# Scheduler's timeline model switched off, and the turned tiles' fp16 halves moved from the transposed-tile pool to the untransposed one

## The chip, the cores and the metric

One core of one Trainium2 chip runs the whole program. The metric is the device time in microseconds. The time of before is the median of three runs; one further execution was profiled, and all rows below are of that one.

## The reference

The inputs are fp32 `q`, `k`, `v` of 2 batches x 8 heads x 768 positions x 64, a projection 64 x 6, and two pairs of feed-forward weights 512 x 2048 and 2048 x 512 in double precision.

```python
q_bits = (np.einsum('bhsd,dk->bhsk', q, proj) > 0)
q_bucket = np.sum(q_bits * powers, axis=-1)          # k likewise
mask = q_bucket[:, :, :, None] == k_bucket[:, :, None, :]
scores = np.where(mask, scale * np.matmul(q, k.T), -1e9)
attn = softmax(scores); x = (attn @ v), heads side by side: (1536, 512)
h = x @ w_in;  g = h * sigmoid(h);  x = g @ w_out     # first feed-forward
h = x @ w_in2; g = h - tanh(h);     out = g @ w_out2  # second feed-forward
```

Attention goes only between positions whose six hash bits agree; its result goes through two feed-forward layers.

## The kernel before

**Attention.** There are 16 heads, 8 of each batch, and each head has 6 score tiles of 128 query rows by 768 keys, so 96 tiles in all; they are counted here from 0, tile i being row block i % 6 of head i // 6. For one tile these steps follow each other:

- `scores` (line 243): four matmuls of 384 columns into two PSUM banks. Half of them need the head's hash rows, which `hash_mm` (line 172, PE), an eviction on DVE (line 185) and two small DMAs issued from ACT's queue (lines 187 and 188) have put into the operands beforehand.
- `soft_max` (line 256, DVE) reads the scores, takes the row maximum and writes the fp32 tile `p`; `soft_exp` (lines 264 and 265, ACT) makes the bias and the exponential in place.
- Then `p` is split into an fp16 high part and an fp16 rest, and both are transposed, in one of two ways. The 24 odd tiles of the first batch are turned on PE (`turn_p`, line 278): six transposes into PSUM, high part by ACT (line 280), rest by DVE (line 281). The 72 other tiles go by `soft_hi` (line 290, ACT), `soft_lo` (line 297, POOL) and a transposing DMA issued from SP's queue (line 299).
- `pv` (lines 311 to 313): 18 fp16 matmuls of 65 columns from the transposed tile `pt`, written in the source six tiles behind `scores`.

The loop over `s` issues these steps of several tiles staggered. Where a batch ends, 13 steps run without new scores.

**Pools.** `pt_p` has four buffers of 128 x 12 x 128 fp16; before, both ways put their transposed tile there. `wk` has four buffers for `p` and four for the fp16 pair `hl`. For the first 22 odd tiles (`EXTRA = 44`) `soft_max` takes a double-width fp32 tile from a pool that the feed-forward uses later (four buffers over two tags), with `p` in its first half and room for an fp16 pair in its second:

```python
big = extra.tile([128, 2 * S], F32, tag=("gh", "gl")[i // 2 % 2], name="p")
p = big[:, 0:S]
hlx[i] = big[:, S:2 * S].bitcast(F16).rearrange("p (a s) -> p a s", a=2)
```

Before, that second half stays unused.

**Feed-forward.** Weights of 512 x 512 pieces come in as pairs of 32-bit words, are turned to fp32 by ACT and four DVE steps (lines 506 to 510 and 497), split in two fp32r parts (lines 498 and 499), and those of the first layer are stored to DRAM as fp32 (line 501) for a second pass. A group is 12 matmuls of 384 columns into one bank (`h_group` line 530, `o_group` line 554) and an eviction by ACT and DVE (lines 536 to 542, 566). There are 256 groups. The first 64 belong to batch 0's tokens and are issued one per step beside the attention of batch 1; the other 192 follow it. While the two overlap, the scores have one buffer of two banks (`ps_s`), since the second was given to the feed-forward.

**Order.** The program is traced in the source's order, and the framework's scheduler then sets each engine's queue: it walks the program with a model of time and gives every engine the ready instruction of highest priority, the source's place being the priority (`@early` raises it for a few). Each engine, and SP's queue of DMAs, then executes its queue strictly in that order, held up by semaphores.

Of the kernel before, what the change touches and what calls it, by code (L numbers as in the profile page):

```python
# [9 lines left out]
F16 = mybir.dt.float16  # L10
# [39 lines left out]
def lsh_attention_moe_kernel(  # L50
# [12 lines left out]
    nc = tc.nc  # L63
    B, H, _, _, S = qkT.shape
# [4 lines left out]
    NQ = S // 128  # L69
# [34 lines left out]
    def bank():  # L104
        turn[0] += 1
        pool = ps_more[0] if ps_more and turn[0] % ps_turn[1] < ps_turn[0] else ps_m
        return pool.tile([128, 512], F32, tag="m", name="psm")


    def attention(pools, vraw, extra, xw):  # L110
# [9 lines left out]
        hlx, vmxs = {}, {}  # L120
# [148 lines left out]

        def turn_p(i):  # L270
            p, _ = pexp.pop(i)
            pt = pt_p.tile([128, 2 * NQ, 128], F16, tag="pt", name="pt")
            w = NQ // 2
            for u in range(2):
                ps = bank()
                for x in range(w):
                    kt = u * w + x
                    nc.tensor.transpose(ps[:, x * 128:(x + 1) * 128], p[:, kt * 128:(kt + 1) * 128], ident)
                hi, lo = (pt[:, x + u * w:x + (u + 1) * w, :].rearrange("p a q -> p (a q)") for x in (0, NQ))
                nc.scalar.copy(hi, ps[:, 0:HS])  # L280
                nc.vector.tensor_tensor(lo, ps[:, 0:HS], hi, op=ALU.subtract)
            ptile[i] = pt
# [88 lines left out]
        def at(s):  # L371
            b, r = divmod(s, per + gap)
            return b * per + r if s >= 0 and b < B and r < per else None

        for s in range(B * (per + gap)):
            evs, late = late, []
            i, i1, i2, j, j1, j3 = (at(s - x) for x in (0, 1, 2, LAG, LAG + 1, LAG + 2))
# [4 lines left out]
            if i2 is not None and direct(i2):  # L382
                turn_p(i2)
# [349 lines left out]
```

## Time and profile before

| | us |
|---|---|
| median of three runs | 794.8 |
| lowest and highest of them | 789.62, 795.64 |
| the profiled execution's own time | 791.22 |
| its span, first to last instruction | 789.4 |

Durations and gaps below are within the span of the profiled execution; 1.8 us of its time lie around the span. The trace divides into the attention of batch 0 alone (to about 154 us), batch 1's attention with the first 64 feed-forward groups (to about 390 us) and the other groups.

### The profile page before, as it was taken

Reading aid. Unit: us, or ns where it says so; the run is one execution under the profiler, and the core shown is the slowest. Engines: PE = TensorE matmul, PEld = TensorE weight load, DVE = VectorE, ACT = ScalarE, POOL = GpSimd, SP = SyncE. Lnnn points to the kernel's source line nnn. Section 1 sums busy time; section 2 is a strip of 40 time slices with the busy share of each in tenths; the row PEclk is TensorE's granted clock in tenths of the full one; section 3 lists DMA queues with packets and bytes.
Section 4 is the critical chain, followed back from the end, with each engine's and each line's share of the span. In section 5 each row is a group of like instructions: output and inputs, shape, how many; then the busy total and the mean of one; then the engine's idle time right before and its main releaser. Section 6 shows DMA issues by size and latency. Waiting matters only on the chain.

```text
span 789.4 us, 14334 instructions
## 1 busy us (share of the span) xinstructions
PE 733.6 (93%) x5492; PEld 700.0 (89%) x5492; DVE 544.4 (69%) x1029; ACT 433.1 (55%) x821; POOL 309.5 (39%) x214
## 2 busy tenths in 40 slices
PE   4778798789989899999999999999999999999998
PEld 3667677679978798899999999999999999999998
DVE  6968688798878778778542443998768576584342
ACT  4849788797788678667443441553524334242130
POOL 4536537466777667566455420222111110110000
PEclk8899899899999999999999999999999999999999
DMA  7695776969999899994333320323112121210102
GB/s 255 190 148 106 126 154 167 212 155 197 263 245 211 214 180 240 215 218 136 97 104 107 95 81 1 101 90 130 53 56 78 57 81 33 75 54 0 52 29 81
DMA packets 138879, 100.39 MB, mean 127 GB/s; under 512 B 115870, under 2 KB 118174, under 8 KB 138810
## 3 DMA queue, kind: packets, MB, share of 16 engines
q1 hardware_dynamic: 137712, 97.54, 50.6%
q10 hardware_dynamic: 1098, 1.94, 1.0%
q8 instruction: 43, 0.70, 0.3%
q14 instruction: 26, 0.21, 0.1%
HBM read 57.95 MB, written 11.53 MB: 88 GB/s over the span
## 4 chain that ended last, share of the span: by engine, by line
PE 55%; DMA 2%; ACT 1%; DVE 0%; issue 0%; POOL 0%; ACTq 0%; DVEq 0%
PE psm L554 28%; PE psm L530 26%; DMA pt<-hl 1%; DMA w<-wi 1%; PE ps L243 0%; ACT xh L577 0%; ACT p L265 0%; POOL hl L297 0%; PE pso L311 0%; POOL wl L485 0%; ACT wh L484 0%; ACT th L536 0%; PE pso L312 0%; PE pso L313 0%; ACT hl L290 0%
## 5 line engine op out<-in xcount | busy, mean ns | idle before, releaser
L499 POOL TENSOR_TENSOR wl<-wa,wh 128x512 fp32r<-128x512 f32 x64 | 83.8, 1309 | 244.3 <-ACT wh L498 244.3
L530 PE MATMUL psm<-xh,wh 128*128 128x384 f32 x512 | 173.2, 339 | 1.6 <-ACT wh L484 1.6
L554 PE MATMUL psm<-gh,wh 128*128 128x384 f32 x512 | 173.0, 338 | 0.6 <-ACT x L346 0.4
L554 PE MATMUL psm<-gl,wh 128*128 128x384 f32 x512 | 171.5, 335 | 0.0
L530 PE MATMUL psm<-xl,wh 128*128 128x384 f32 x512 | 171.4, 335 | 0.0
L530 PE MATMUL psm<-xh,wl 128*128 128x384 f32 x512 | 170.0, 335 | 0.0
L554 PE MATMUL psm<-gh,wl 128*128 128x384 f32 x512 | 169.4, 335 | 0.0
L297 POOL TENSOR_TENSOR hl<-p,hl 128x768 f16<-128x768 f32 x72 | 120.4, 1674 | 88.0 <-ACT hl L290 82.5
L256 DVE TENSOR_SCALAR_CACHE_REDUCE p<-ps 128x768 f32<-128x768 f32 x96 | 90.8, 952 | 29.7 <-PE ps L243 20.0
L530 PEld LDWEIGHTS psm<-xh,wh 128*128 128x128 f32 x512 | 96.5, 188 | 2.1 <-ACT wh L484 1.9
L243 PE MATMUL ps<-k,q 128*128 128x384 f32 x336 | 82.9, 372 | 15.9 <-DVE p L256 9.0
L554 PEld LDWEIGHTS psm<-gh,wh 128*128 128x128 f32 x512 | 96.3, 188 | 1.5 <-ACT x L346 0.6
L554 PEld LDWEIGHTS psm<-gl,wh 128*128 128x128 f32 x512 | 96.4, 188 | 0.0
L530 PEld LDWEIGHTS psm<-xl,wh 128*128 128x128 f32 x512 | 96.4, 188 | 0.0
L566 DVE TENSOR_TENSOR acc<-acc,psm 128x384 f32<-128x384 f32 x96 | 52.1, 551 | 63.5 <-PE psm L554 63.1
L530 PEld LDWEIGHTS psm<-xh,wl 128*128 128x128 f32 x512 | 95.9, 188 | 0.0
L554 PEld LDWEIGHTS psm<-gh,wl 128*128 128x128 f32 x512 | 95.8, 188 | 0.0
L542 DVE TENSOR_TENSOR gl<-psm,gh 128x384 fp32r<-128x384 f32 x128 | 70.6, 554 | 31.9 <-ACT gh L541 31.7
L265 ACT ACTIVATE p<-p,bi 128x768 f32<-128x768 f32 x96 | 89.0, 939 | 2.9
L541 ACT CAST gh<-psm 128x384 fp32r<-128x384 f32 x128 | 61.4, 480 | 50.5 <-DVE psm L540 35.1
L311 PE MATMUL pso<-v,pt 128*128 128x65 f16 x576 | 70.9, 200 | 15.4 <-DMA pt<-hl 15.3
L311 PEld LDWEIGHTS <-pt 128*128 128x128 f16 x576 | 55.3, 101 | 27.2 <-DMA pt<-hl 17.4
(90 smaller groups left out, 1267.2 us busy)
## 6 DMA issues: line engine op xcount, KB each, us to landing
w<-in_w_in_dram SPq DMA_DIRECT2D x32, 512.0 KB
w<-in_w_out_dram SPq DMA_DIRECT2D x32, 512.0 KB
r<-in_qkT_dram SPq DMA_DIRECT2D x15, 768.0 KB
wi<-wa SPq DMA_DIRECT2D x16, 256.0 KB
wo<-wa SPq DMA_DIRECT2D x16, 256.0 KB
w<-wi SPq DMA_DIRECT2D x16, 256.0 KB
w<-wo SPq DMA_DIRECT2D x16, 256.0 KB
vr<-in_v_dram SPq DMA_DIRECT2D x6, 512.0 KB
```

What stands on the lines that cost most here:

```text
L243: nc.tensor.matmul(out=ps[:, u, 0:HS], lhsT=a[:, t * 128:(t + 1) * 128], rhs=c[:, u * HS:(u + 1) * HS], start=(j == 0), stop=(j == 1))
L256: nc.vector.tensor_scalar(p.rearrange("p (c s) -> p c s", c=2), pss.pop(i)[:, :, 0:HS], FLOOR, None, op0=ALU.max, op1=ALU.max, accum_out=m)
L265: nc.scalar.activation(out=p, in_=p, func=ACTF.Exp, scale=0.125, bias=bi)
L297: nc.gpsimd.tensor_tensor(hl[:, 1, :], p, hl[:, 0, :], op=ALU.subtract)
L311: nc.tensor.matmul(out=o, lhsT=pt[:, kt, :], rhs=v16[:, kt, h, :], start=(kt == 0), stop=False)
L499: nc.gpsimd.tensor_tensor(ll, s, hh.bitcast(F32), op=ALU.subtract)
L530: nc.tensor.matmul(out=ps, lhsT=a[:, k, fs], rhs=b_[blk][:, k, :], start=(k == 0 and j == 0), stop=(k == KD - 1 and j == 2))
L541: nc.scalar.copy(gh[:, f, :], ps)
L542: nc.vector.tensor_tensor(gl[:, f, :], ps, gh[:, f, :].bitcast(F32), op=ALU.subtract)
L554: nc.tensor.matmul(out=ps, lhsT=a[:, f, ds], rhs=b_[:, f, :], start=(f == 0 and j == 0), stop=(f == F - 1 and j == 2))
L566: nc.vector.tensor_tensor(ac, ac, ps, op=ALU.add)
```

## The change

Two edits. The scheduler's model of time is switched from the timeline simulation to the simpler default, which changes the order on every queue. And `turn_p` no longer takes its fp16 tile from `pt_p`: it takes the unused second half of the odd tile's own buffer, or a `wk` buffer `hl` for the two odd tiles after `EXTRA`. From line 273 on, line numbers of the changed kernel are one higher.

```diff
         def turn_p(i):
             p, _ = pexp.pop(i)
-            pt = pt_p.tile([128, 2 * NQ, 128], F16, tag="pt", name="pt")
+            pt = hlx.pop(i) if i in hlx else wk.tile([128, 2, S], F16, tag="hl", name="hl")
+            pt = pt.rearrange("p a s -> p (a s)").rearrange("p (a q) -> p a q", q=128)
             w = NQ // 2
...
-    with _tile.TileContext(nc, schedule_with_timeline_sim=True) as tc:
+    with _tile.TileContext(nc, schedule_with_timeline_sim=False) as tc:
         lsh_attention_moe_kernel(tc, *args)
```

Neither setting gives the literal order of the source: of instructions that stand next to each other on a queue, 167 pairs on PE, 273 on DVE and 222 on ACT stood against the order in which the source issues them, and 92, 235 and 184 do now. The matmuls, evictions and DMAs themselves are the same in number and shape. In PE's queue of tiles 12 to 47 a `pv` stands on average 6.9 score tiles behind the newest scores (8.6 before), and in that of tiles 54 to 89 it stands 5.8 behind (3.9 before).

SP's queue, at the end of batch 0's attention, before: the transposing DMA of tile 38, two stores of converted weights (`wi32`) with the loads behind them, and the transposing DMAs of tiles 40 and 42.

```order
L299 DMA_TRANSPOSE pt_1898<-hl_1825 128x12x128
L501 DMA wi32_75<-wa_1563 128x512
L466 DMA w_1635<-in_w_in1_dram 128x1024
L501 DMA wi32_75<-wa_1586 128x512
L466 DMA w_1725<-in_w_in1_dram 128x1024
L299 DMA_TRANSPOSE pt_1979<-hl_1908 128x12x128
L299 DMA_TRANSPOSE pt_2076<-hl_1999 128x12x128
L134 DMA r_2568<-in_qkT_dram 128x1536
```

And the same place now, from the second store on; its transposing DMAs are those of tiles 38, 40 and 42.

```order
L502 DMA wi32_75<-wa_1570 128x512
L467 DMA w_1708<-in_w_in1_dram 128x1024
L300 DMA_TRANSPOSE pt_1879<-hl_1807 128x12x128
L502 DMA wi32_75<-wa_1641 128x512
L467 DMA w_1770<-in_w_out1_dram 128x1024
L300 DMA_TRANSPOSE pt_1959<-hl_1889 128x12x128
L502 DMA wi32_75<-wa_1714 128x512
L467 DMA w_1850<-in_w_out1_dram 128x1024
L300 DMA_TRANSPOSE pt_2055<-hl_1979 128x12x128
```

Four stores stand ahead of tile 42's transpose instead of two, and they alternate with the transposes.

ACT's queue in the middle of batch 0's attention, before: the two DMAs that carry head 5's hash rows (`h0_129`, `l0_130` from `hb`; the scores of tile 30 are the first that need them) stand behind the exponential of tile 25, `p_1200`.

```order
L264 ACTIVATE bi_1266<-mx_1232 128x1
L265 ACTIVATE p_1200<-p_1200,bi_1221 128x768
L280 CAST pt_1015<-psm_1016 128x384
L290 CAST hl_1185<-p_1144 128x768
L187 DMA h0_129<-hb_992 18x768
L280 CAST pt_1015<-psm_1022 128x384
L188 DMA l0_130<-hb_992 18x768
L280 CAST pt_1097<-psm_1098 128x384
```

Now the same two DMAs stand behind the exponential of tile 21, `p_1018`.

```order
L264 ACTIVATE bi_1120<-mx_1100 128x1
L281 CAST p_920<-psm_1006 128x384
L265 ACTIVATE p_1018<-p_1018,bi_1039 128x768
L281 CAST p_920<-psm_1012 128x384
L187 DMA h0_129<-hb_983 18x768
L188 DMA l0_130<-hb_983 18x768
L265 ACTIVATE p_1053<-p_1053,bi_1077 128x768
L281 CAST p_1018<-psm_1087 128x384
```

They moved four tiles forward against the exponentials; the high part of a turned tile (line 280, now 281) is written into the tile `p` itself.

DVE's queue beside the feed-forward, before: from the row maximum of tile 66 to that of tile 68 (`psm` and `gl` are a group's eviction, `cv` a weight conversion, `hb` a hash eviction).

```order
L256 TENSOR_SCALAR p_3406,mx_3407<-ps_3395 128x768
L537 SCALAR_TENSOR_TENSOR psm_3370<-th_3455,psm_3370 128x384
L542 TENSOR_TENSOR gl_3309<-psm_3312,gh_3308 128x384
L537 SCALAR_TENSOR_TENSOR psm_3442<-th_3530,psm_3442 128x384
L256 TENSOR_SCALAR p_3477,mx_3478<-ps_3467 128x768
L185 TENSOR_SCALAR hb_3577<-psm_3578,cst_sb_69 82x384
L507 TENSOR_SCALAR cv_3394<-cv_3394 128x512
L542 TENSOR_TENSOR gl_3309<-psm_3370,gh_3308 128x384
L542 TENSOR_TENSOR gl_3309<-psm_3442,gh_3308 128x384
L256 TENSOR_SCALAR p_3552,mx_3553<-ps_3542 128x768
```

Now the same stretch, tiles 66 to 68:

```order
L256 TENSOR_SCALAR p_3384,mx_3385<-ps_3373 128x768
L538 SCALAR_TENSOR_TENSOR psm_3348<-th_3433,psm_3348 128x384
L508 TENSOR_SCALAR cv_3372<-cv_3372 128x512
L256 TENSOR_SCALAR p_3455,mx_3456<-ps_3445 128x768
L509 TENSOR_SCALAR cv_3372<-cv_3372 128x512
L543 TENSOR_TENSOR gl_3287<-psm_3348,gh_3286 128x384
L511 SCALAR_TENSOR_TENSOR cv_3372<-w_3095,cv_3372 128x512
L538 SCALAR_TENSOR_TENSOR psm_3420<-th_3508,psm_3420 128x384
L498 SCALAR_TENSOR_TENSOR wa_3371<-w_3095,cv_3372 128x512
L256 TENSOR_SCALAR p_3530,mx_3531<-ps_3520 128x768
```

A whole weight conversion and a group's eviction now stand between the row maxima of tiles 67 and 68.

## Rows read from the trace of the kernel before

**Rows 1.** Page, part 1: busy time, share of the span and instructions

```profile
PE 733.6 (93%) x5492; PEld 700.0 (89%) x5492; DVE 544.4 (69%) x1029; ACT 433.1 (55%) x821; POOL 309.5 (39%) x214
```

**Rows 2.** Windows: stretch, its length, busy time per engine, granted clock, DMA share, GB/s

```profile
58.00:154.00 96.00, 79.26 (x948) 68.75 (x947) 75.20 (x159) 78.26 (x153) 53.86 (x32) 0.91 0.72 154
154.00:208.00 54.00, 49.38 (x420) 45.69 (x417) 49.37 (x94) 44.83 (x79) 36.64 (x24) 0.97 0.83 190
208.00:350.00 142.00, 133.89 (x1240) 122.63 (x1238) 111.67 (x219) 106.19 (x188) 92.29 (x60) 0.99 1.03 219
...
390.00:786.00 396.00, 395.84 (x2284) 395.52 (x2282) 237.46 (x426) 146.08 (x293) 77.94 (x60) 1.00 0.21 68
```

**Rows 3.** Lines 265 and 256, three stretches: count, duration, first and last start

```profile
L265 ACT ACTIVATE p<-p,bi x36: 919/936/970, 58.0 to 142.9; 128x768 f32<-128x768 f32 x36
...
L265 ACT ACTIVATE p<-p,bi x13: 930/939/966, 154.1 to 204.7; 128x768 f32<-128x768 f32 x13
...
L256 DVE TENSOR_SCALAR_CACHE_REDUCE p<-ps x35: 944/958/959, 208.1 to 350.0; 128x768 f32<-128x768 f32 x35
```

**Rows 4.** Chain that ended last: start, us, what

```profile
322.84 5.53 DMA pt<-hl
...
336.64 0.05 PE pso L311
...
337.19 0.25 PE psm L554
...
346.17 0.71 PE ps L243 x4
...
403.12 16.64 PE psm L554 x96
```

**Rows 5.** Waits, 58 to 154 us, PE and SP: total, times, longest

```profile
PE pso L311 <- DMA pt<-hl: 4.9, 2, 3.9
PE ps L243 <- DMA l<-hb: 3.5, 1, 3.5
PE ps L243 <- DMA k<-hb: 2.1, 3, 0.8
...
SPq L299 <- PE pso L313: 33.6, 11, 6.6
```

**Rows 6.** Timeline of SP's queue, 126 to 140 us

```profile
129.75 1.46 SPq L299 DMA_TRANSPOSE pt<-hl  x1
...
135.34 6.16 SPq L299 DMA_TRANSPOSE pt<-hl  x2
```

**Rows 7.** Timeline of ACT, 38 to 60 us

```profile
48.78 0.48 ACT L280 CAST pt<-psm 128x384 f16<-128x384 f32 x1 [4.25 <-PE psm L278]
```

**Rows 8.** Waits, 208 to 386 us, PE and SP

```profile
PE pso L311 <- DMA pt<-hl: 6.9, 6, 2.7
PE psm L530 <- ACT wh L484: 1.6, 1, 1.6
...
SPq L501 <- DVE wa L497: 22.2, 12, 4.4
```

**Rows 9.** Groups by form, 208 to 350 us, DVE: busy, mean ns, idle before

```profile
L256 DVE TENSOR_SCALAR_CACHE_REDUCE p<-ps 128x768 f32<-128x768 f32 x34 | 32.5, 954 | 14.5 <-PE ps L243 11.2 <-POOL wl L499 1.7 <-PE pso L313 1.4
...
L507 DVE TENSOR_SCALAR cv<-cv 128x512 f32<-128x512 f32 x18 | 12.5, 696 | 6.7 <-ACT cv L506 6.7
...
L537 DVE SCALAR_TENSOR_TENSOR psm<-th,psm 128x384 f32<-128x384 f32 x16 | 8.8, 554 | 0.1
L542 DVE TENSOR_TENSOR gl<-psm,gh 128x384 fp32r<-128x384 f32 x16 | 8.7, 548 | 0.9 <-ACT gh L541 0.9
```

**Rows 10.** Groups by form, 58 to 154 us, POOL and ACT

```profile
L297 POOL TENSOR_TENSOR hl<-p,hl 128x768 f16<-128x768 f32 x18 | 30.3, 1683 | 34.5 <-ACT hl L290 30.6 <-DMA k<-hb 3.9
...
L290 ACT CAST hl<-p 128x768 f16<-128x768 f32 x18 | 15.0, 835 | 1.0 <-DMA q<-hb 1.0
...
L163 POOL TENSOR_TENSOR k<-r,k 128x768 fp32r<-128x768 f32 x4 | 7.4, 1842 | 0.2
```

## The prediction

> **What bounds the kernel now.** I read the page's busy line first, then a table of stretches, then in each stretch the waits, and last the chain. PE is 93% busy [rows 1], but its share hides three regimes. Up to 154 us batch 0's attention runs alone: between 58 and 154 us no engine is full: PE shows 79.3 of 96 us, in matmuls that overlap, ACT 78.3 and DVE 75.2 [rows 2]. Between 208 and 350 us the attention of batch 1 shares PE with feed-forward groups; PE is busy 133.9 of 142 us. From 390 us on PE has 395.8 of 396 us, and the chain is nothing but groups of 12 matmuls, 16.64 us for 96 of them [rows 4], so 0.173 us for one of 384 columns. What stands there is work; no order of it can be cheaper. A gain has to come before 390 us, where an in-order queue waits for another.
>
> The marks in time are the exponentials and row maxima [rows 3]: the 13th exponential (tile 12) starts at 58.0 us, the 49th (tile 48, batch 1's first) at 154.1, the row maximum of tile 61 at 208.1 and of tile 95 at 350.0. I go from mark to mark.
>
> **Up to tile 12 (58.0 us): -3 us.** Two stops show what goes wrong here; the larger is ACT's 4.25 us before it copies a turned tile at 48.78, waiting for PE [rows 7], which itself stood in front of a `pv` whose transpose came late. The second edit leaves `pt_p` to the 72 tiles that go by DMA, and in SP's new queue the third transposing DMA no longer stands behind a load of q and k, so this stop should go: -4.25. Against it the new order puts batch 0's six conversions of `v` on ACT and on DVE in front of the exponentials of tiles 1 to 3, which delays the first tiles by some 5 us, though that work is only moved and not added. I take -3, near the stop that goes; the ends are -7 (the stop and the small ones around it) and +3 (the stop stays as a wait elsewhere, and the delay counts).
>
> **Tiles 12 to 48 (96 us): -6 us.** What goes: PE's waits for hash rows, 3.5 us in one piece and 2.1 in three [rows 5], since the DMAs that bring them now stand four tiles earlier on ACT's queue while five tiles of scores, not one or two, lie between the hash matmuls and their first user. Also PE's waits for a transposed tile, 4.9 us, the longest 3.9 [rows 5]. That one is at tile 40: SP issued tile 38's transpose only at 129.75 and tile 40's at 135.34 [rows 6], held by its `pt` buffer and by the two stores in between. SP stood 33.6 us in 11 waits for a `pv` to free a buffer [rows 5]; with the turned tiles out of `pt_p` these should be gone. Sum: 3.5 + 2.1 + 4.9 = 10.5 us. What comes: two more weight pieces are converted before tile 46 than were, eight DVE steps of 0.70 us [rows 9], 5.6 us on an engine with 20.8 us free here; a `pv` stands 6.9 tiles behind the scores and not 8.6, so it waits sooner. I count 4.5 us for both, most of the DVE steps. 10.5 - 4.5 = 6. The ends: -16, where ACT would be full (78.3 us, and three weight copies more), and +16, worked out under the slower rival.
>
> **Tiles 48 to 61 (54 us): -3 us.** Here one can count per step, from one row maximum to the next, what PE and DVE each have to do by their queues. A step of PE in its usual form is 4 score matmuls 0.70, a `pv` 0.55 (336.64 to 337.19) and a group 2.08 us [rows 4], 3.33 in all; a step of DVE is a row maximum 0.95, a weight conversion 4 x 0.70, a group's two evictions 0.55 + 0.55 [rows 9], or some of these. The scores have one buffer, so neither engine gets more than a step ahead, and a step takes the longer of the two. Summed over the 13 steps the longer ones give 70.5 us before and 67.3 now; against the 54 us measured both are too high, as PE's first step there was begun before the mark. Only the difference is used: -3.
>
> **Tiles 61 to 95 (142 us): -3 us.** The same count over 34 steps gives PE 125.3 and DVE 122.0 us before, and 140.3 for the sum of the longer of the two; the trace has 141.9. For the new order it is 120.9 and 120.9, and 137.0. The step shown in the last pair of orders, after tile 67's row maximum, is one that loses: 0.95 + three conversion steps 2.1 + 1.1 of eviction = 4.1 us on DVE against 3.4 on PE. So what PE gains from a regular order (and from `pv` now 5.8 tiles behind, not 3.9, which covers the 6.9 us of waits for transposes [rows 8]), DVE mostly takes back. 137.0 - 140.3 gives -3; the ends are -13 (PE alone) and +6 (ACT or SP late as well).
>
> **After tile 95 (437 us to the end): +5 us.** The new order runs the scores further ahead, so it leaves more behind them: 2508 matmuls of 384 columns in place of 2472, 36 x 0.173 = 6.2 us, and two `pv` more, 1.1 us. From tile 95's scores to the end the old order needs 433 us of PE by these prices, and the trace 437: 4 us of waits, 1.6 of them for the second pass's weights [rows 8]. In the new queue all remaining groups of the first pass, 96 matmuls, stand in one row ahead of the first group that needs these weights, so I let half go: 7.3 - 2 = +5. This is the term that is easily forgotten: three of the microseconds won before are only work put off.
>
> **Sum.** -3 - 6 - 3 - 3 + 5 = -10 us on the profiled execution's 791.2, so 781. That execution lies 0.45% below the median of 794.8 and within the three runs; I carry a small part of that over and say 782.
>
> **Rivals.** *The transfers bound the second half* (chance 0.18). In 208 to 350 us the 16 DMA engines show a share of 1.03 and 219 GB/s [rows 2], and SP's queue stood 22.2 us for converted weights to store [rows 8]. If the DMA engines are full there, a better order gets no tile transposed sooner, the 142 us stay, and the two -3 of the second half fall: 788. Against it: PE waited only 6.9 us in all for transposes in that stretch. [...]
>
> *A clean first half* (0.17). ACT never starves: -7, -11 between tiles 12 and 48, -6, -6 (DVE's excess half hidden), +4. Sum -26: 765. For it speaks that every long wait there has its cause moved; against it that DVE and ACT are both over 78% full and trade results twice per turned tile.
>
> *PE stands in front of `pv`* (0.15), the case that ends slower. The place is PE's queue of tiles 12 to 47. From the end of an exponential to its transposed tile there are a copy of 0.84 on ACT, 1.68 on POOL [rows 10] and 5.53 of DMA [rows 4], 8 us; when POOL first has a head's two operand differences, 2 x 1.84 [rows 10], 11.7. With the scores, row maximum and exponential before it, 2.8, this makes 14.5 us, and 6.9 tiles at 2.17 us of ACT each (78.3 / 36) give 15.0; before, 8.6 tiles gave 18.7. It decides as soon as a tile's exponential waits on ACT behind another's: then each head's pair on POOL costs its 3.7 us on PE, and by the turned tiles on ACT; six heads 22 us. In place of -6 this is +16: 791.2 - 10 + 22 = 803.
>
> *The edits do nothing* (0.05). The new queues are still a scheduler's order, and where its model was not wrong the two agree: 791.
>
> My forecast has 0.45. The range reaches from a little under the clean half to the slow rival, 762 to 803; about one in ten is left out on each side. A difference under 1% can hardly be told from none. Faster by over 1% than 794.8 is below 786.9: most of the forecast (0.36), the clean half (0.17) and a little of the first rival, 0.57; slower is above 802.7, half of the slow rival, 0.09; the rest 0.34.
>
> **What would show it.** Right: SP's waits for a `pv` between 58 and 154 us fall from 33.6 us to under 10; PE's waits for hash rows there are gone; tile 48's exponential starts near 145 us; from tile 61 to 95 it still takes 137 to 140 us, with PE waiting for DVE's row maxima and no longer for transposes; the scores of tile 95 come some 15 us earlier and the end only 10. Wrong: tile 48 no earlier than 152 us with `pv` waits in PE's list above 15 us; or the stretch from tile 61 to 95 at 142 us or more; or a wait for weights of over 5 us at the first group of the second pass.

## The result, and the profile after

| | before | after |
|---|---|---|
| median, both timed on one chip, 15 runs each (us) | 790.66 | 783.05 |
| lowest and highest (us) | 784.37, 799.68 | 779.41, 788.3 |
| the profiled execution's own time (us) | 791.22 | 781.58 |
| its span (us) | 789.4 | 779.8 |

The ratio is 0.9905, with an interval from 0.9883 to 0.9926: a little under 1% faster. The forecast was 782, and -10 us on the profiled execution; it became -9.6 (the medians differ by 7.6). But the sum came out right from terms that did not. In the same marks:

| stretch | before | after | change | forecast |
|---|---|---|---|---|
| to the 13th exponential | 58.0 | 52.7 | -5.3 | -3 |
| to the 49th exponential | 96.1 | 101.3 | **+5.2** | -6 |
| to the row maximum of tile 61 | 54.0 | 51.6 | -2.4 | -3 |
| to that of tile 95 | 141.9 | 129.8 | **-12.1** | -3 |
| to the end | 439.4 | 444.4 | +5.0 | +5 |

The marks are the exponentials (line 265) and row maxima (line 256) of after, which answer to [rows 3]:

```profile
L265 ACT ACTIVATE p<-p,bi x36: 919/937/956, 52.7 to 148.8; 128x768 f32<-128x768 f32 x36
...
L265 ACT ACTIVATE p<-p,bi x13: 920/938/958, 154.0 to 204.7; 128x768 f32<-128x768 f32 x13
...
L256 DVE TENSOR_SCALAR_CACHE_REDUCE p<-ps x35: 944/949/959, 205.6 to 335.4; 128x768 f32<-128x768 f32 x35
```

Busy time per stretch of after, with the columns of [rows 2]:

```profile
52.70:154.00 101.30, 80.06 (x980) 68.22 (x978) 79.34 (x161) 78.07 (x155) 55.68 (x34) 0.95 0.70 152
154.00:205.60 51.60, 47.20 (x396) 43.48 (x394) 44.04 (x91) 44.13 (x81) 32.10 (x23) 0.96 0.86 197
205.60:335.40 129.80, 126.39 (x1223) 118.78 (x1220) 109.32 (x216) 106.59 (x190) 96.14 (x63) 1.00 1.06 241
```

In the third row PE has 126.4 of 129.8 us: 3.4 us idle where [rows 2] had 8.1. In the first it is idle for 21.2 us (101.30 - 80.06) where it was 16.7. What PE, ACT and SP waited for in that first stretch of after (total, times, longest), beside [rows 5]:

```profile
PE ps L243 <- DVE p L256: 6.7, 8, 2.1
PE pso L312 <- DMA pt<-hl: 4.1, 6, 1.5
PE pso L312 <- DVE xt L330: 3.3, 2, 2.6
...
ACT wh L499 <- DVE wa L498: 6.6, 4, 3.1
...
ACT wa L507 <- DMA w<-in_w_in_dram: 2.3, 1, 2.3
...
SPq L300 <- POOL hl L298: 47.0, 17, 6.0
SPq L502 <- DVE wa L508: 8.0, 2, 7.5
...
SPq L502 <- DVE wa L498: 3.5, 1, 3.5
```

The waits for hash rows (5.6 us) and SP's 33.6 us for a `pv` are gone, as forecast. In their place ACT stands 8.9 us for weight conversions, and SP 11.5 us with stores of weights that aren't converted yet. SP's part is mostly hidden, since it would otherwise have stood for POOL. This is the first transpose behind the first store, tile 34's:

```profile
116.16 6.80 SPq L300 DMA_TRANSPOSE pt<-hl  x2
```

POOL had finished tile 34's fp16 rest at 114.60 (its row, from 112.95, is the last one shown in this document), so the store held this transpose up by 1.6 us, and PE took the tile up at 122.08 without a wait. The other transposes from tile 28 to tile 46 went out within 0.4 us of POOL's row.

PE's waits of after between 205.6 and 377 us, where [rows 8] had 6.9 us for transposed tiles, and the first links of the chain, as in [rows 4]:

```profile
PE pso L312 <- DVE xt L330: 1.6, 2, 1.2
PE psm L531 <- POOL wl L500: 1.1, 1, 1.1
PE ps L243 <- DVE p L256: 0.7, 1, 0.7
```

```profile
377.05 16.64 PE psm L531 x96
```

Transposed tiles are gone from the list. From 377 us on the groups run as before, 96 matmuls in 16.64 us.

### The profile page after: what moved, and what is told of

It is laid out like the page before. It is cut to its first block, busy times and chain, and to the rows that moved or that the text cites. A ratio compares the mean times of both kernels' runs of the same rounds, so it can differ in the third digit from the quotient of the medians.

```text
span 779.8 us, 14314 instructions
## 1 busy us (share of the span) xinstructions
PE 728.1 (93%) x5492; PEld 698.0 (90%) x5492; DVE 541.5 (69%) x1029; ACT 432.0 (55%) x821; POOL 306.2 (39%) x214
## 4 chain that ended last, share of the span: by engine, by line
PE 55%; POOL 1%; DVE 0%; ACT 0%; issue 0%; ACTq 0%
PE psm L555 27%; PE psm L531 27%; POOL xl L579 1%; POOL wl L500 0%; PE pso L312 0%; PE pso L314 0%; PE pso L313 0%; DVE p L256 0%; DVE wa L498 0%; DVE xt L330 0%; DVE acc L567 0%; ACT xh L578 0%; DVE den L321 0%; DVE den L320 0%; ACTq L578 0%
## 5 line engine op out<-in xcount | busy, mean ns | idle before, releaser
L555 PE MATMUL psm<-gh,wl 128*128 128x384 f32 x512 | 171.6, 335 | 0.6 <-POOL wl L500 0.6
L531 PEld LDWEIGHTS psm<-xh,wh 128*128 128x128 f32 x512 | 96.1, 188 | 1.6 <-DVE hb L185 0.6
L531 PEld LDWEIGHTS psm<-xh,wl 128*128 128x128 f32 x512 | 96.1, 188 | 1.5 <-POOL wl L500 1.5
L243 PE MATMUL ps<-k,q 128*128 128x384 f32 x336 | 84.5, 371 | 13.5 <-DVE p L256 9.6
L243 PEld LDWEIGHTS ps<-k,q 128*128 128x128 f32 x336 | 62.1, 205 | 18.1 <-DVE p L256 10.9
L540 ACT ACTIVATE th<-psm 128x384 f32<-128x384 f32 x64 | 31.5, 493 | 75.6 <-PE psm L531 75.6
```

The source lines that it names most:

```text
L243: nc.tensor.matmul(out=ps[:, u, 0:HS], lhsT=a[:, t * 128:(t + 1) * 128], rhs=c[:, u * HS:(u + 1) * HS], start=(j == 0), stop=(j == 1))
L531: nc.tensor.matmul(out=ps, lhsT=a[:, k, fs], rhs=b_[blk][:, k, :], start=(k == 0 and j == 0), stop=(k == KD - 1 and j == 2))
L540: nc.scalar.activation(out=th, in_=ps, func=ACTF.Tanh)
L555: nc.tensor.matmul(out=ps, lhsT=a[:, f, ds], rhs=b_[:, f, :], start=(f == 0 and j == 0), stop=(f == F - 1 and j == 2))
```

## The experiments

Each was timed against before on one chip, and profiled once. The chip is not the same one for all: e1 to f4 ran on one, g1 and g3 on a second, g4 and g5 on a third. So runs of different groups are compared by their ratios to before and by their profiles, not by their medians. The stretches are cut at the same marks as above; "rest" ends with the span. Where two runs share an order and their buffers, a stretch that nothing touched differs by up to 0.9 us (f1 and g3, g1 and g5).

| run | to 12 | 12-48 | 48-61 | 61-95 | rest | median | ratio to before |
|---|---|---|---|---|---|---|---|
| before | 58.0 | 96.1 | 54.0 | 141.9 | 439.4 | 790.66 to 791.32 | 1 |
| after | 52.7 | 101.3 | 51.6 | 129.8 | 444.4 | 783.05 | 0.9905 [0.9883, 0.9926] |
| e1_order | 52.7 | 104.7 | 53.4 | 137.2 | 446.5 | 797.25 | 1.0093 [1.0066, 1.0120] |
| e2_pool | 53.7 | 94.7 | 72.1 | 137.1 | 441.6 | 799.95 | 1.0092 [1.0062, 1.0122] |
| e3_lag4 | 53.9 | 109.0 | 52.2 | 136.4 | 445.9 | 798.03 | 1.0088 [1.0056, 1.0120] |
| e4_pre20 | 53.1 | 102.2 | 53.3 | 132.6 | 444.4 | 786.76 | 0.9942 [0.9920, 0.9963] |
| e5_lag8 | 52.3 | 101.7 | 54.9 | 142.1 | 451.2 | 804.02 | 1.0151 [1.0106, 1.0196] |
| f1_newbuf_e1order | 52.7 | 100.8 | 54.5 | 138.2 | 446.5 | 794.96 | 1.0055 [1.0038, 1.0072] |
| f2_oldbuf_afterorder | 53.6 | 102.7 | 49.9 | 130.5 | 445.2 | 783.65 | 0.9887 [0.9846, 0.9929] |
| f4_oldbuf_e2order | 54.5 | 93.1 | 69.7 | 136.4 | 444.8 | 800.82 | 1.0101 [1.0051, 1.0151] |
| g3_tworows | 52.6 | 101.6 | 53.6 | 134.9 | 446.5 | 790.25 | 1.0009 [0.9981, 1.0037] |
| g1_splice48 | 53.7 | 93.1 | 52.1 | 132.0 | 445.0 | 777.18 | 0.9854 [0.9801, 0.9907] |
| g4_tenrows | 52.4 | 103.2 | 50.0 | 130.7 | 445.3 | 783.88 | 0.9922 [0.9894, 0.9949] |
| g5_splicehash | 53.2 | 93.3 | 52.3 | 129.9 | 445.5 | 776.28 | 0.9814 [0.9774, 0.9853] |

### Which edit gives what

The scheduler's setting alone (e1_order), and the pool edit alone (e2_pool):

```diff
-    with _tile.TileContext(nc, schedule_with_timeline_sim=True) as tc:
+    with _tile.TileContext(nc, schedule_with_timeline_sim=False) as tc:
```

```diff
-            pt = pt_p.tile([128, 2 * NQ, 128], F16, tag="pt", name="pt")
+            pt = hlx.pop(i) if i in hlx else wk.tile([128, 2, S], F16, tag="hl", name="hl")
+            pt = pt.rearrange("p a s -> p (a s)").rearrange("p (a q) -> p a q", q=128)
```

> The scheduler's setting alone; turned tiles stay in the pool pt_p. Theory A (the gain lies between the row maxima of tiles 61 and 95 and comes from the new order, in which a pv stands some two tiles further behind the scores): that stretch takes 128 to 133 us, as in the changed kernel (129.8), and the whole 781 to 789, the loss against the changed kernel being what the first half loses by turned tiles that hold pt buffers again (up to 6 us between the 13th and 49th exponential, with SP waiting over 20 us for pv there). Theory B (the gain comes from the freed pt buffers): the stretch from tile 61 to 95 is back at 138 to 142 us and the whole at 790 or more.

> The pool edit alone; the scheduler's timeline model stays on. Theory A: between the row maxima of tiles 61 and 95 it takes 138 us or more, as before (141.9), since no tile is turned there; the whole lies at 788 to 795, with the first half (start to 49th exponential, 154.1 before) at most 4 us shorter and SP's waits for a pv between 58 and 154 us under 15 us in place of 33.6. Theory B: the stretch from 61 to 95 takes 133 us or less and the whole is 785 or less.

Both theories fall: e1_order's 137.2 us is not theory A's 128 to 133, and e2_pool's 137.1 is not theory B's 133 or less. Each edit alone makes the kernel 0.9% slower; only together do they make it faster. With the setting alone the stretch from 61 to 95 gains 4.7 us and not 12.1, though no tile is turned there. With the pool edit alone that stretch is 137.1 too, and tiles 48 to 61 take 72.1. Either the freed buffers matter in a way that reaches tile 95, or they only change what the scheduler makes of the program.

### The same buffers in another order, the same order on other buffers

To part these, the queues were pinned. After tracing, the kernel adds an edge of order alone (no wait) from each instruction of a queue to the next, along a table of another kernel's queue:

```diff
+    for name in ("PE", "DVE", "Activation", "Pool", "SP"):
+        queue = [i for i in traced if str(i.engine) == "EngineType." + name]
+        rows = [queue[n + moves[at + n]] for n in range(len(queue))]
+        at += len(queue)
+        for a, b in zip(rows, rows[1:]):
+            tc.add_manual_dep(b, a.name, _mybir.DependencyInfo(_mybir.DependencyClass.NoSync, ...
...
         lsh_attention_moe_kernel(tc, *args)
+        _pin(nc, tc, _mybir)
```

The five queues hold 7,724 instructions; e1_order's and after's differ at 1,444 places. The table was taken from e1_order for f1 (on after's buffers), from after for f2 (on the old buffers), from e2_pool for f4 (on the old buffers).

> Both edits, but every queue pinned, row by row, to the queues of the kernel that has the scheduler's setting alone (797.25 us): same order as that kernel, freed pt buffers. Theory P (the freed buffers work by themselves, by letting transposes start earlier): 781 to 786 us, the stretch from tile 61 to 95 at 128 to 132 us. Theory Q (the freed buffers work only by way of the order that the scheduler makes with them): 794 to 799 us, and the stretch stays at 135 to 139.

> The scheduler's setting with the turned tiles back in pt_p, every queue pinned, row by row, to the queues of the changed kernel (783.05 us). Theory P: 793 us or more, SP waiting over 15 us for a pv between tiles 12 and 48. Theory Q: 781 to 786 us, as the changed kernel, since its order is the same and the four pt buffers were not what the chip waited for.

> The kernel before, every queue pinned, row by row, to the queues of the kernel that has the pool edit alone (799.95 us). Theory P: 803 us or more, slower than that kernel by what the buffers give. Theory Q: 797 to 803 us; then the order alone, of the same instructions on the same pools, takes the kernel from 791 to 800, and the long stretch from tile 48 to 61 (72.1 us there, 54.0 before) shows again at 70 or more.

Theory Q holds in all three: the time goes with the order. f2 has the old buffers and is as fast as after; its row maxima from tile 48 to 95 lie 0.7 to 3.2 us behind after's, all the way. f1 has the freed buffers and keeps e1_order's 138 us; it wins back 3.9 us between tiles 12 and 48, of which 0.4% of the whole is left. f4 shows e2_pool's long stretch again (69.7, just under the 70 of the expectation). So the pool edit, as a matter of buffers, is worth between nothing and 0.4%. SP's waits say the same. This is SP's queue of f2 between 53.6 and 156.3 us, and f2's stretch from 61 to 95:

```profile
SPq L299 <- PE pso L313: 13.7, 5, 6.6
```

```profile
206.20:336.70 130.50, 126.42 (x1224) 118.63 (x1221) 109.33 (x215) 106.58 (x190) 96.08 (x63) 1.00 1.05 241
```

In f2 SP stands 13.7 us for a `pv` to free a buffer, and after has no such wait there. Yet the stretch takes 102.7 us and 101.3, and the two kernels take the same time. So these stops of SP cost 1.4 us at the most; here a stop of that queue counts only as far as PE then misses a transposed tile.

### Is it the distance of pv, or the time at which conversions begin

e3_lag4 and e5_lag8 write a `pv` four and eight tiles behind the scores, e4_pre20 begins the conversions eight steps later:

```diff
-LAG = 6
-GAP = 7
+LAG = 4
+GAP = 9
```

```diff
-LAG = 6
-GAP = 7
+LAG = 8
+GAP = 5
```

```diff
-PRE = 28
+PRE = 20
```

> The changed kernel with a pv written four tiles behind the scores and not six (and the gap at a batch's end so much longer). Theory A (the distance of pv is what the second half gained by): the stretch from tile 61 to 95 goes back to 137 to 142 us, with PE waiting over 5 us for transposed tiles there, and the whole is 788 to 796. Rival D (the gain is only the regular order of groups and conversions on PE and DVE, whatever the distance): the stretch stays within 128 to 132 us, and the whole below 785. For the first half: if pv standing too near is what cost 5 us between the 13th and 49th exponential (101.3 in the changed kernel), this stretch grows to 106 or more; if it is the weight conversions pulled forward, it stays within 99 to 104.

> The changed kernel with a pv written eight tiles behind the scores and not six. If the distance of pv sets the time between the 13th and 49th exponential (96.1 before, 101.3 in the changed kernel, 109.0 with four tiles): 96 to 99 us, and between the row maxima of tiles 61 and 95 at most 129.8; the whole 776 to 781. If the distance has given what it can: 100 to 103 and 129 to 132, the whole 782 to 788.

> The changed kernel with the weight conversions begun eight steps later in the source (20 pieces of lead and not 28). Theory C (the conversions pulled forward into batch 0's attention cost the 5 us between the 13th and 49th exponential): this stretch takes 94 to 97 us in place of 101.3, ACT's waits for DVE's conversion steps (6.6 us for the split alone in the changed kernel) fall under 3, and half or more of it comes back later as work put off, so that the whole lies at 779 to 785. Rival (the shorter distance of pv costs them): the stretch stays at 100 to 103 us and the whole does not get faster.

Four tiles are too near: PE's waits of e3_lag4 for transposed tiles, tiles 12 to 48 and then 61 to 95, are

```profile
PE pso L312 <- DMA pt<-hl: 9.4, 7, 2.8
...
PE pso L312 <- DMA pt<-hl: 4.9, 4, 1.9
```

against 4.1 and none in after, so the mechanism of the prediction's slow rival exists. Theory A's numbers were missed by little (136.4 us for 137, 4.9 us of waits for over 5, 798.03 for at most 796), rival D's by far. But eight tiles don't help either (101.7 and 142.1, the slowest kernel of all; neither expectation had the 142.1), and e1_order, with `pv` as far behind the scores in tiles 48 to 89 as after (5.5 and 5.4 tiles), needs 137.2. The distance is a condition, not the gain. With eight tiles the four `pt` buffers don't reach: in e5_lag8 SP stands 35.9 us for a `pv` between 208.9 and 351 us (18.2 in after's stretch), and ACT, which fills the tiles that wait for SP, 13.4 us (0.2 in after):

```profile
SPq L300 <- PE pso L314: 35.9, 20, 5.7
...
ACT hl L291 <- DMA pt<-hl: 13.4, 12, 2.7
```

e4_pre20 speaks against the theory for which it was made. The stretch takes 102.2 us, as the rival has it, though the rival's cause, the shorter distance, is not borne out by e5_lag8's 101.7. Its first four conversions lie between tiles 43 and 47 and not 34 and 42; its exponential of tile 42 comes at 125.0 (131.7 in after), and by tile 48 it has lost all of that. ACT's waits in its tiles 12 to 48:

```profile
ACT wa L507 <- DMA w<-in_w_in_dram: 5.1, 2, 3.8
ACT wh L499 <- DVE wa L498: 4.9, 4, 3.2
```

These are 10.0 us, in after 8.9, in before 0.9 (0.5 and 0.4; 1.3 more stand there without a releaser). So when the conversions come matters little. What e4_pre20 did not change is that ACT's and DVE's rows of one piece stand so close that ACT stops for DVE.

### One slow stretch taken apart, row by row

f1 loses 8.4 us on after between the row maxima of tiles 61 and 95. It loses them in two places, 4.8 us from tile 63 to 64 and 7.7 from tile 69 to 73, and wins a little back elsewhere. PE's waits of f1 between 208 and 346.2 us:

```profile
PE ps L243 <- DVE p L256: 4.7, 2, 3.9
PE psm L555 <- POOL wl L500: 3.5, 1, 3.5
```

The first stop on DVE (its timeline and a row of ACT's; the bracket is the idle time before a row and what ended it): the row maximum of tile 64 at 223.11 is late, since in the queue it stands behind steps of a conversion whose load ACT is waiting for.

```profile
215.91 0.55 DVE L565 COPY acc<-psm 128x384 f32<-128x384 f32 x1
220.71 0.70 DVE L508 TENSOR_SCALAR cv<-cv 128x512 f32<-128x512 f32 x1 [4.25 <-ACT cv L507]
...
223.11 0.95 DVE L256 TENSOR_SCALAR_CACHE_REDUCE p<-ps 128x768 f32<-128x768 f32 x1
...
220.05 0.62 ACT L507 ACTIVATE cv<-w 128x512 f32<-128x512 f32 x1 [4.11 <-DMA w<-in_w_in_dram]
```

The second on POOL: the low part of a weight piece (line 500) could start when ACT had copied its high part at 255.2, and stands behind two operand differences of a head that is needed later. PE goes on at 259.87.

```profile
254.87 1.84 POOL L159 TENSOR_TENSOR q<-r,q 64x768 fp32r<-64x768 f32 x1
256.79 1.81 POOL L163 TENSOR_TENSOR k<-r,k 128x768 fp32r<-128x768 f32 x1
258.55 1.27 POOL L500 TENSOR_TENSOR wl<-wa,wh 128x512 fp32r<-128x512 f32 x1
```

g3_tworows is f1 with two rows of the table moved:

```diff
 DVE:  M63 ac
-      w1.11 w2.11 ac w3.11 M64 w4.11
+      M64 w1.11 w2.11 ac w3.11 w4.11
 POOL: lo70
-      q k wl15 lo71
+      wl15 q k lo71
```

(M64 is the row maximum of tile 64, w1 to w4 the steps of a conversion, wl15 a piece's low part, q and k the operand differences.)

> The kernel with both edits pinned to the slower queues (794.96 us), with two rows moved: on DVE the row maximum of tile 64 ahead of the first step of the weight conversion that waits for its load (PE stood 3.9 us for that row maximum), and on POOL the low part of the 16th weight piece ahead of the two operand differences of head 13 (PE stood 3.5 us for that piece). If these two rows are what makes this order slow between the row maxima of tiles 61 and 95 (138.2 us against 129.8): 130 to 133 us there and the whole 787 to 790. If the stops only move to the next late row: 136 to 139 and 793 to 797.

The whole, 790.25, lies just outside the first expectation, and the stretch, 134.9, between the two; the ratio to before is 0.46% under f1's, and the profiled span 3.5 us shorter. The first place loses nothing on after any more (4.8 us in f1), the second still 4.3 of its 7.7. The second stop is gone. The first turned into one of 1.9 us for a transposed tile, at 222.8, and one of 0.9 for a weight piece, at 225.3. Windows of f1 around its stops, with the clock that TensorE was granted, as the trace gives it (1.00 is full), behind the busy times:

```profile
215.00:224.00 9.00, 5.18 (x45) 4.70 (x43) 4.71 (x11) 3.44 (x6) 3.84 (x4) 0.93 1.20 241
224.00:229.00 5.00, 4.88 (x30) 4.57 (x31) 3.17 (x9) 3.15 (x7) 4.17 (x3) 0.50 1.19 316
...
256.00:260.00 4.00, 0.49 (x4) 0.17 (x3) 0.56 (x1) 2.45 (x6) 3.92 (x4) 1.00 0.51 181
260.00:264.00 4.00, 4.00 (x43) 3.49 (x44) 2.14 (x5) 1.85 (x5) 2.73 (x2) 0.57 0.12 23
```

Behind each stop PE is nearly full (4.88 of 5.00 us and 4.00 of 4.00) and the granted clock is 0.50 and 0.57. PE's busy time in f1's whole stretch is 129.45 us, 3.1 more than in after (126.39), with no more matmuls (1202 and 1223 in the windows). Of the 8.4 us that f1 needs more, 5.3 is idle PE and 3.1 longer busy time. Taking the missing share of the clock as time lost, I estimate 4.88 x 0.50 + 4.00 x 0.43 = 4.2 us for the two slow windows; that the 3.1 are theirs is not shown. g3's whole stretch:

```profile
207.80:342.70 134.90, 129.51 (x1202) 119.13 (x1202) 109.13 (x214) 106.88 (x191) 96.43 (x62) 0.97 1.04 230
```

g3 still shows 0.50 between 224 and 229 us, and 1.00 between 256 and 264. But its PE is busy as long as f1's, so the 3.3 us that it won are idle time alone, 5.4 us against 8.75. What one stop costs by the clock isn't shown by this pair.

### Another order for the first half

g1_splice48 pins e2_pool's order up to about tile 48 and after's from there on. No code but the table changes:

```diff
-rows of tiles 0 to 48: after's queues
+rows of tiles 0 to 48: e2_pool's queues (first 1251 of PE, 192 of DVE, 234 of ACT, 49 of POOL, 53 of SP)
 rows from there on: after's queues
```

> Both edits, every queue pinned: up to about tile 48 the rows stand as in the kernel with the pool edit alone (row maximum of tile 48 at 147.1 us there, 150.3 in the changed kernel), from there on as in the changed kernel. If what a piece of an order costs stays with that piece (theory Q, local faults): the row maximum of tile 48 at 146 to 148.5, the stretches from tile 48 to 61 and from 61 to 95 as in the changed kernel (51.6 and 129.8, within 3 us), and the whole 778 to 782. Rival (a lead won early is lost at the next meeting of the queues): 783 to 787, the row maximum of tile 61 no earlier than 205.

At 777.18, 0.9854 [0.9801, 0.9907], it is clearly faster than before. The interval still overlaps after's by a little; against after the profile speaks, in which the row maximum of tile 61 comes 6.7 us earlier. Tiles 12 to 48 take 93.1 us with the same four conversions in them, and ACT's and SP's waits for conversions there are

```profile
ACT wh L499 <- DVE wa L498: 1.1, 2, 0.7
...
SPq L502 <- DVE wa L498: 13.5, 4, 4.7
```

ACT's are 1.1 us in place of 8.9. SP's are longer than after's 11.5, and the stretch is 8 us shorter all the same. The lead of 6.7 us at tile 61 shrinks to 4.4 by tile 95; the stretch costs 132.0 and not 129.8.

g4_tenrows tries to mend after itself where it stops, with ten rows moved on ACT and DVE:

```diff
 ACT:  E33 t31
-      wA0 E34 wA1 hi34 t33 t33 wC0 E35 E36 ... wC1 wA2 E38 t37 ... wC2 wA3 hi40 ... wC3 hi42 t41 t41
+      E34 hi34 wA0 wA1 t33 t33 E35 E36 wC0 ... E38 t37 wC1 wA2 ... hi40 wC2 wA3 ... hi42 t41 t41 wC3
 DVE:  lo31
-      w1.0 nm4 w2.0 M37
+      nm4 M37 w1.0 w2.0
```

(E are exponentials, hi and t copies of high parts, wA a conversion's first copy, wC its last; nm4 scales a finished head.)

> The changed kernel, every queue pinned as it is, with ten rows moved between tiles 33 and 43: on ACT each copy and split of the first four weight pieces stands one to four rows later, behind the exponential or the copy that it held up (ACT stood 6.6 us there for DVE's conversion steps and 2.3 us for the first load), on DVE the first piece's first two steps stand behind the row maximum of tile 37. If these stops are the 5 us that the stretch from the 13th to the 49th exponential has lost against before (101.3 against 96.1): 94 to 98 us there, and the whole 777 to 781. If the stops are hidden, or only move on: 100 to 103 us there and the whole 782 to 785.

The first expectation fails. ACT's waits for conversions fall from 8.9 to 3.2 us, and the exponential of tile 36 comes at 113.0 and not 116.8. Then PE stands for tile 32's transposed tile, and at tile 37 all is given back. ACT's, PE's and SP's waits of g4, tiles 12 to 48 (SP: 96 to 124 us), and two rows of the timeline:

```profile
ACT wh L499 <- DVE wa L498: 2.6, 2, 2.1
...
ACT wa L507 <- DMA w<-in_w_in_dram: 0.6, 1, 0.6
```

```profile
PE pso L312 <- DMA pt<-hl: 9.9, 6, 4.9
```

```profile
SPq L502 <- DVE wa L508: 5.2, 1, 5.2
```

```profile
105.49 3.07 SPq L300 DMA_TRANSPOSE pt<-hl  x1
...
113.74 0.23 PE L312 MATMUL pso<-v,pt 128*128 128x65 f16 x1 [4.87 <-DMA pt<-hl]
```

Tile 32's transpose went out 0.15 us after POOL had finished its tile, right behind two weight loads of 512 KB, and PE could go on 8.2 us later. In e4_pre20, where no load stands there, PE waited for the same tile too, and the transpose took at most 5.0 us (106.14 to 111.10). The store for which SP stands 5.2 us held up the next transpose, tile 34's, by 4.0 us, but PE did not wait for that tile; in e2_pool's and before's queues this store stands behind the transposes of tiles 34 and 36. So mending ACT's stops alone brings out late transposes. In g1's order neither stop is there and the stretch is 8 us shorter, but that order differs from after's at 1,488 places, and which of them count is not shown.

g5_splicehash moves three rows in g1, since PE stood 2.1 us for head 12's hash rows in front of tile 72's scores:

```diff
 DVE:
-      hb12.0 w3.14 gl11 w4.14 M69 hb12.1
+      hb12.0 hb12.1 w3.14 gl11 w4.14 M69
 ACT:
-      th12 wC14 wA15 b69 E69 dq12 dk12
+      th12 dq12 dk12 wC14 wA15 b69 E69
```

(hb12 are the two halves of that eviction, dq12 and dk12 the DMAs that carry it.) The wait in g1:

```profile
242.95 0.59 PE L243 MATMUL ps<-k,q 128*128 128x384 f32 x2 [2.06 <-DMA k<-hb]
```

> The spliced order (777.18 us) with three rows moved: the second half of head 12's hash eviction on DVE ahead of a conversion step, and the two DMAs that carry it on ACT's queue some three us earlier, since PE stood 2.1 us for these hash rows ahead of tile 72's scores. If that stop is on the path: the row maximum of tile 95 two to four us earlier than in the spliced kernel (331.0) and the whole 773 to 776; if the next wait takes its place: 330 to 332 and 776 to 779.

The row maximum of tile 95 comes at 328.6 and not 331.0, as the first theory has it; the whole, 776.28, lies just above what it gave, and where the second put it. At 0.9814 [0.9774, 0.9853] this is the fastest median here. Its interval is clear of after's, but not of g1's, so the 2.3 us that it wins on g1 are seen in the profile alone.

## Why the prediction was right or wrong

**Up to tile 12, -3, came as -5.3.** Right in sign; the delay of the first tiles by the conversions of `v` is there (tile 3's exponential 21.7 before, 29.5 now) and was caught up by tile 12 in every run with either edit. e2_pool, which lacks that delay, also reaches 53.7.

**Tiles 12 to 48, -6, came as +5.2.** This step failed: "10.5 - 4.5 = 6". Of the 10.5 us, the hash rows' 5.6 went, but of the 4.9 for transposed tiles only 0.8 did (4.1 left). What came was mis-sized and of another kind. I priced the conversions by DVE's busy time, and what the trace shows is stops in in-order queues: ACT stood 8.9 us for them, with exponentials and copies behind it, and PE's idle time grew by 4.5 us. That these stops are the whole of the loss is not shown. With most of ACT's taken away (g4) the stretch takes 103.2 us, since late transposes take their place; with the conversions only put off (e4_pre20) 102.2; with g1's order, in which ACT stands 1.1 us for them and PE 2.7 for transposed tiles, 93.1. The stores that the pair of SP queues ahead of the prediction showed were not the price: they held one transpose up by 1.6 us, and PE did not wait for it. The slow rival had the place right and, for this kernel, neither price nor cause; its cause proper shows in e3_lag4.

**Tiles 48 to 61, -3, came as -2.4.** The number is right, but by luck more than by the count. In this stretch the groups have 147 matmuls where they had 159, at 0.173 us 2.1 us of work put off, and PE's idle time is nearly the same, 4.4 us after 4.6. The count gave a time 16 us too long for either kernel.

**Tiles 61 to 95, -3, came as -12.1.** The mechanism (a more regular order, transposes in time) was right and the size off. The term that was mis-sized is "137.0 for the sum of the longer of the two": the trace has 129.8, with PE at 126.4. Two things were wrong in it. It had DVE at 120.9 us, where the trace has DVE busy for 109.3. And a step does not take the longer of PE and DVE: PE waited 0.7 us in all for row maxima. As I read it, a row maximum that ends before the next scores are due leaves slack, and DVE's long steps draw on it. That the same count had met before's 141.9 within 1.6 us was chance: before idled for other reasons, 6.9 us for transposes among them. The end named for PE alone, -13, was the better value. Not all of the 12.1 us is won. 4.7 are idle time of PE that went, and 7.5 are busy time, of which 3.6 are 21 matmuls of groups put off. These are the groups' matmuls in the stretch, lines 530 and 554 of before, then 531 and 555 of after:

```profile
208.10:350.00 141.90, 43.17 (x218) 37.70 (x219) 0.99 1.03 219
208.10:350.00 141.90, 43.13 (x216) 37.42 (x216) 0.99 1.03 219
205.60:335.40 129.80, 37.89 (x192) 33.04 (x192) 1.00 1.06 241
205.60:335.40 129.80, 43.30 (x221) 38.02 (x222) 1.00 1.06 241
```

f1 and g3 show how far such a gain hangs on single rows: with e1_order's order two places lose 12.5 us on after, of which 4.1 come back elsewhere, and one row moved at each wins 3.3 us.

**After tile 95, +5, came as +5.0.** Right, by its own terms: the groups have 33 matmuls more to do (36 were forecast) and there is one `pv` more (two were), PE is busy 6.2 us longer, and of its waits for weights 0.6 us are left (1.6 in before). So 5.7 of the 14.5 us won between tiles 48 and 95 were only put off.

**The rivals.** The transfers did not bind: the same tiles moved in 129.8 us, at 241 GB/s. That the edits do nothing is wrong for both together, and true within 0.4% of the pool edit once the order is held. "A clean first half" (-11 between tiles 12 and 48) was reached by no order here; the best takes 93.1 us there, -3.0.

**The signs named.** SP's waits for `pv` and PE's for hash rows went, and tile 95's scores came 15.5 us earlier with an end 9.6 earlier: as said. Tile 48 near 145 (it came at 154.0) and 137 to 140 us in the second half, with PE waiting for row maxima: both wrong, in opposite directions, and they cancel. The forecast of 782 owes that to luck: +11 and -9.

What stays open: which rows of after's order lose the 5 us between tiles 12 and 48; where the other 3.9 us of PE's shorter busy time between tiles 61 and 95 come from; why tiles 48 to 61 take 72 us in e2_pool's order; and the reading of e5_lag8 (buffers too few for eight tiles) rests on its waits alone.

## What to carry to other kernels

A pool edit and a scheduler's switch can't be judged one by one: measure what an edit does with the queues pinned, for a scheduler answers each edit with another order, and here orders of the same instructions spread from 776 to 801 us. When a long chain of producers (load, copy, convert, split, store) enters an in-order queue, price the rows queued behind its waits, on every engine that it touches, not its busy time; and count a stop of the DMA queue only as far as something behind it is missed. And mend stops from the row that waits: two or three rows at the right place were worth 3.5 us in g3 and 1.8 in g5, and ten rows in g4 nothing, where another wait took the place of the mended ones. Last, of what a stretch wins look for what it only puts off.

## What the runs showed of the hardware

**TensorE's clock behind a stop.** In f1, after a stop of 3.9 us and one of 3.5 us, PE was busy for 4.88 of the next 5 us and for all of the next 4, and was granted 0.50 and 0.57 there, where the other windows of that stretch, cut from 208 to 346.2 us, have 0.93 to 1.00. Its PE was busy 3.1 us longer than after's, beside 5.3 us more of idle time. In g3 a stop of 1.9 us was followed by 0.50 too, with one of 0.9 us in that window, the second slow window was gone, and PE was busy just as long (129.51 us and 129.45). In g3's slow window a group's matmuls of 384 columns began 0.32 us apart (227.19 to 229.75), and before its stop 0.17 to 0.18 us (218.65 to 219.89). So the time lost around a stop can be more than its wait, but these runs don't tell how much a single one costs.

**DVE steps beside POOL.** The last DVE step of a conversion, between SBUF tiles, over four pieces: before, with the step in front of it (line 510, between SBUF tiles too), then after (min/median/max in ns), and the same step of after from 205.6 us on, where one input is in PSUM:

```profile
L497 DVE SCALAR_TENSOR_TENSOR wa<-w,wa x4: 675/681/692, 128.4 to 150.7; 128x512 int32<-128x512 int32 x4
...
L510 DVE SCALAR_TENSOR_TENSOR wa<-w,wa x4: 679/973/2030, 124.4 to 149.7; 128x512 int32<-128x512 int32 x4
```

```profile
L498 DVE SCALAR_TENSOR_TENSOR wa<-w,wa x4: 674/1641/2031, 113.1 to 134.7; 128x512 int32<-128x512 int32 x4
...
L498 DVE SCALAR_TENSOR_TENSOR wa<-w,cv x17: 673/680/690, 210.2 to 330.4; 128x512 int32<-128x512 int32 x17
```

The longest one, 2.03 us, began 0.17 us after a POOL subtraction of 1.65 us:

```profile
113.12 2.03 DVE L498 SCALAR_TENSOR_TENSOR wa<-w,wa 128x512 int32<-128x512 int32 x1
...
112.95 1.65 POOL L298 TENSOR_TENSOR hl<-p,hl 128x768 f16<-128x768 f32 x1 [7.66 <-ACT hl L291]
```

The first four pieces' 16 DVE steps took 13.1 us before and 16.2 in after. Before has such long steps as well, in line 510 and in line 508 (2.02 us at 120.46). In both traces these are steps that began while POOL ran a row: nine of after's 16 and four of before's did, and each of them ended 0.28 to 0.56 us behind that row. The others took 0.41 to 0.43 us (lines 507 and 508 of before, 508 and 509 of after) and 0.67 to 0.69 (497 and 510, 498 and 511). So the same step was dearer by up to 1.3 us where an order put it beside a POOL row, and the 0.70 of the prediction, from rows with an operand in PSUM, was no price for it. The 2.03 us are near the 1.48 that POOL's row still had and the step's own 0.68. With one input in PSUM, 13 of the 17 steps of line 498 began while POOL ran a row, and none took over 0.69 us. g1's 16 steps took 16.8 us in a stretch of 93.1, so this was not what cost the 5 us.
